# Re-ordering the steps of a fused layernorm, long-convolution and gated-GLU kernel

## The chip, the cores and the metric

The kernel runs on one core of a Trainium2 chip. Its time is the device time of one execution in microseconds (us); the figure for a kernel is the median of several executions. Five engines work side by side on a core: PE (TensorE, matrix products), DVE (VectorE), ACT (ScalarE), POOL (GpSimd) and SP (SyncE, which here issues nearly all the transfers). Each has a queue of instructions of its own and works it off strictly in order; semaphores hold an instruction back until what it needs is done. The profile also shows PEld, the loading of weights into TensorE, and the DMA engines that move the data.

## The reference

The input has 2048 rows and 640 channels, in bf16. Cut to what matters:

```python
xn = layernorm(A_q)                                   # over the 640 channels
# A: a shift convolution and a long convolution, per channel
k_shift[t] = sum over m<4 of k[t-m] * shift_k[:, m]
kv = k_shift * v
y  = irfft(rfft(kv, 4096) * rfft(ssm_k, 4096))[:2048] + kv * ssm_D
A  = xn * y
# B: a gated GLU, 640 -> 1728 -> 640
B  = (sigmoid(xn @ w_gate) * (xn @ w_up)) @ w_down
out = A_q + A + B
```

## The kernel before, in words

**Rows and the GLU.** Row 16p + b lies on partition p, in block b (16 blocks of 128 rows). Blocks form four groups t of 512 rows. For a group, the layernorm runs on DVE (`ln_norms`, `ln_var`, `ln_xn`, lines 192 to 219) and POOL (`ln_pow`), and four transposing transfers (`xn_turn`, line 240) write xn, turned, into the one buffer `xnT`. (Group 0 is turned on PE.) Then 13 pairs of `gate_mm` and `up_mm` (line 260, five matmuls each, 128x512) and one `both_mm` (line 281) follow. ACT takes the sigmoid of the gate product (`gate_ev`, line 269; `both_ev`, line 287), and DVE multiplies it with the up product into `hT` (`up_ev`, line 275). Each result lies in one of four PSUM buffers, the pool psG (tag g), and a product must wait until the buffer of four products earlier has been read. At the end of a group stand 16 steps of `down_mm` (line 304, seven matmuls each), two to a result, and `down_ev` (line 309, DVE) adds that into `x`, from which the output is stored.

**The convolution.** It is done in five chunks c of 128 channels, as a two-stage Fourier transform by small matrices. For a chunk:

- `load_k`, `load_halo`, `load_v`, `load_taps`, `load_h` fetch its inputs. `load_h` (lines 134 to 139) fills `hn`, of which there is one buffer, so `load_h(c)` can go only when `h_turn(c-1, ·)` (line 323, DVE, a transposition) has read it.
- `kv_op(c, 0..15)` (lines 330 to 346, DVE) does the shift convolution and the product with v, into `kvh` (two buffers).
- `st1_mm(c, 0..7)` (lines 363 and 365) is the first stage on PE, eight matmuls each, into the pool psC (two PSUM buffers, tag c). `st1_ev` copies the result to an SBUF tile `t1` (two buffers, each for two results): by ACT (line 223) or by DVE (line 226).
- `wr1(c, 0..3)` (line 377) writes a full `t1` to a table in DRAM, 512 KB, "d<-t" in the profile. The `t1` buffer comes free when that write has landed. So `st1_ev(c, 4)` waits for `wr1(c, 0)`, `st1_ev(c, 6)` for `wr1(c, 1)`, and `st1_ev(c+1, 0)` for `wr1(c, 2)`.
- `rd2(s)` (line 387) reads the table back in another layout for each of four subgroups s = 4c to 4c+3; `st2_mm(s)` (line 396) is the second stage and needs both psC buffers; `st2_ev(s, 0..1)` copies both to the slot s mod 3 of `xz`; `prod(s, 0..1)` (lines 409 and 411, DVE: a shuffle, then a product) is the product of the two spectra.
- `inv1_mm(y)` (line 425, 32 matmuls, both psC buffers), y = 2c and 2c+1, takes two slots of `xz` for the way back; its read of slots 2y mod 3 and (2y+1) mod 3 goes by a stride over the slots between them. `inv1_ev(y, 0..1)` copies its results to `ao`, `wr2` (lines 441 and 445) and `rdb` (line 455) go through DRAM once more.
- `inv2_mm(c, 0..3)` (line 464, eight matmuls, a psG buffer each) is the last stage; `inv2_q` (line 469) multiplies by xn and `inv2_x` (line 474) adds to `x`, both on DVE.

**What sets the order.** The program is scheduled by hand. All steps stand in `chains`, one list for each letter, each in its natural order; the string `ORDER` is read letter by letter, and each letter emits the next step of its list. The letters:

| letter | step | engine |
|---|---|---|
| g | gate_mm, up_mm, both_mm, down_mm | PE |
| a, b, c, d | st1_mm, st2_mm, inv1_mm, inv2_mm | PE |
| s | gate_ev, both_ev | ACT |
| u | up_ev, both_mul, down_ev | DVE |
| A, B, C | st1_ev, st2_ev, inv1_ev by ACT | ACT |
| I, F, J | the same three by DVE | DVE |
| k, H, l, q, p | kv_op, h_turn, layernorm, inv2_q and inv2_x, prod | DVE |
| t | taps (from chunk 1) | ACT |
| D, P, Z | add_D, ln_pow, taps(0) | POOL |
| m, n, h, K, V, T | loads (weights and chunks 0 and 1; x and a table; then h, k, v, taps of later chunks) | SP |
| w, r, W, R, e, o | wr1, rd2, wr2, rdb, xn_turn, store | SP |

```python
    left = {k: iter(v) for k, v in chains.items()}
    for k in "".join(ORDER.split()):
        fn, args = next(left[{"F": "B", "J": "C", "I": "A", "Y": "E"}.get(k, k)])
        fn(*args, **({"copy": dve_copy} if k in "FJIY" else {}))
```

An engine thus runs its own letters in the order of the string. What the string says of letters of different engines against each other only sets which buffer use comes first and which dependencies arise. SP is one queue for all the letters of its rows: a transfer that has to wait there holds the issues behind it.

Of the kernel before, what the change touches and what calls it, by code (L numbers as in the profile page):

```python
# [57 lines left out]
def kernel(  # L58
# [569 lines left out]
    step("o", store, NB - 1, NB, 4 * P, DM)  # L628

    ORDER = """  # L630
    mgmmmmgmgmgsummZmgmgsmmgugmssgkmmukgskgugkusgsugkkgkHggmmuskuggkHmssukgmDgggukskgukkksaTmmgauAgmkaAH
    HlglAalAlglmwgautAkagugmggPmwlkgAhglkelauleggkakukkugekAAuuDkHgkuaaekgkwgsATKugkAwgsnkkgskgtuKaKAuka
    gskkgauwgkAlDAakVgglkKkrsakAuwAgakgVsAgalswAkaguKgkkAurbgkBswksHgTBgkbtuguBBpkgawkgslaAgsuKkalupKgrA
    AgkahPlnHsAwugaglVasgkgVpAsTAKukDpuckwglkkCgaCaHAugkAkgkeklubkgrkBBgguuwkgbggkpghtBBrbkegleBgBaauegw
    HAparguVkApauAkgwpADWaugakksAngkugpkwlAsucgsgJlpkCulbrgBKBsgaAuapgpAgrbsFggBussWkukrlpcHgguPCCgbslkV
    ggBuBgbpslBkuBRdpgspgWqqcusdgCgkrkkrCsbqFugqBgubskgBRdwBuagpAaqAdgllWwrsewRpugaqgIaggrpAaAaqupgIqupg
    ddcCgeuqgJebgupegFRuBgqbBpgqBgWpdcrguqqgJqCrubwuwdrgFpBgsbqpggpWpqBugBpscsuJggCurpgbggRFBbsWpdsudupq
    rgBqgqBcqRJsgrpCgsbBuWguBpdspqgbuBBgpqdpsgcgrugCRJqbpggsduBqsBgupgspgWqRqcuJdqgsgCdoqgusqWgudggqgugo
    uRgquRggddouqqgguqddgqqqqoquqggoogouoogouoooo
    """  # L640
    left = {k: iter(v) for k, v in chains.items()}
    for k in "".join(ORDER.split()):
# [33 lines left out]
```

## Time and profile before

| | |
|---|---|
| median of 3 runs | 238.03 us (237.77 to 238.77) |
| the profiled execution: its time, its span | 237.94 us, 236.16 us |
| granted TensorE clock | 1.00 |
| PE busy | 229.1 us, 97% of the span |
| DVE busy | 204.1 us, 86% |
| ACT busy | 121.7 us, 52% |
| POOL busy | 11.5 us, 5% |
| moved by DMA | 56.79 MB, mean 240 GB/s |

The span is the time from the first to the last instruction in the trace of the slowest core; the rest of the execution's time lies around it. In a line of a timeline the columns are start and length in us, engine, line of the kernel, operation, what it writes and reads by the program's tile names, its shape and how many instructions the row holds; in brackets stands how long the engine was idle before and what it waited for. A matmul's end is modelled and overlaps the next one's start, so a step's cost on PE is read from start to start. A line of a window has its bounds and length, the busy time and instruction count of PE, PEld, DVE, ACT and POOL in this order, the granted clock, the share of the DMA engines and GB/s. A line of the waits has the engine and the instruction that waited, what it waited for, the total in us, how many times, and the longest. A line of the DMA issues has the transfer, the queue, how many, the size, and the median time from issue to landing in us. SP's "SPq" rows show an issue's start and how long the issuing took, not the transfer.

### The profile page before, as it was taken

The page shows a single profiled execution, that of the slowest core. Times are in us where ns is not written, and L with a number is a line of the kernel's source. Part 1 is how long each engine was busy: PE and PEld are TensorE (multiplying, and loading weights), DVE is VectorE, ACT ScalarE, POOL GpSimd, SP SyncE. Part 2 cuts the span into 40 slices and gives each one's busy share as a digit, 9 for nine tenths or more (in the row PEclk, how much of TensorE's full clock was granted, in tenths as well). Part 3 has the DMA queues.
Part 4 walks back from the last instruction along what each step waited for, and adds up shares of the span by engine and source line. Part 5 has one row for each costly group of instructions (what it writes and reads, how often), then busy time and mean ns, then how long its engine had stood idle before and what let it go on. Part 6 is the DMA issues. An engine that isn't in the chain of part 4 may idle for free.

```text
span 236.2 us, 5433 instructions
## 1 busy us (share of the span) xinstructions
PE 229.1 (97%) x2205; PEld 131.2 (56%) x2205; DVE 204.1 (86%) x364; ACT 121.7 (52%) x152; POOL 11.5 (5%) x24
## 2 busy tenths in 40 slices
PE   7799999999899899999999999999999999999995
PEld 3664445877355445666754444478664344446772
DVE  3632898999969999999999999899999999988473
ACT  2343323633564897776776777653346367653000
POOL 5210000020100001000100010000000000000000
PEclk9999999999999999999999999999999999999999
DMA  6999999958899999899899996899989879556664
GB/s 211 292 313 237 259 308 299 257 174 163 223 317 269 321 253 270 225 286 217 228 232 321 248 265 186 240 246 271 235 260 284 238 186 255 160 155 177 191 212 134
DMA packets 97183, 56.79 MB, mean 240 GB/s; under 512 B 55878, under 2 KB 91270, under 8 KB 96902
## 3 DMA queue, kind: packets, MB, share of 16 engines
q1 hardware_dynamic: 96214, 55.62, 90.3%
q10 hardware_dynamic: 944, 0.82, 1.1%
q8 instruction: 17, 0.28, 0.5%
q14 instruction: 8, 0.07, 0.1%
HBM read 36.12 MB, written 18.35 MB: 231 GB/s over the span
## 4 chain that ended last, share of the span: by engine, by line
PE 84%; DVE 8%; DMA 4%; issue 1%; ACT 0%; ACTq 0%; DVEq 0%
PE pg L260 23%; PE pu L260 23%; PE pd L304 20%; PE psb L464 4%; PE ps L396 3%; DMA w<-in_B_w_up_dram 3%; PE ps L363 3%; PE ps L365 3%; PE psa L425 2%; PE pg L281 1%; DVE st L198 1%; DVE tmp L341 1%; DMA xnT<-xn 1%; DVE acc L343 1%; PE pu L251 1%
## 5 line engine op out<-in xcount | busy, mean ns | idle before, releaser
L260 PEld LDWEIGHTS <-w 128*128 128x128 bf16 x500 | 46.5, 98 | 55.8 <-issue 6.8
L304 PE MATMUL pd<-wd,hT 128*128 128x320 bf16 (+2 forms) x448 | 65.3, 299 | 0.0
L260 PE MATMUL pg<-xnT,w 128*128 128x512 bf16 x250 | 62.2, 380 | 0.9 <-DMA xnT<-xn 0.9
L260 PE MATMUL pu<-xnT,w 128*128 128x512 bf16 x250 | 62.2, 380 | 0.8 <-DVE hT L275 0.8
L304 PEld LDWEIGHTS <-hT 128*128 128x128 bf16 x448 | 41.9, 98 | 18.2 <-issue 2.3
L223 ACT CAST t<-ps 128x1024 bf16<-128x1024 f32 x38 | 37.8, 1016 | 23.6 <-PE ps L365 16.0
L269 ACT ACTIVATE sig<-pg 128x512 bf16<-128x512 f32 x52 | 31.1, 603 | 30.7 <-PE pg L260 27.7
L223 ACT CAST xz<-ps 128x1024 bf16<-128x1024 f32 x35 | 34.2, 1015 | 20.3 <-PE ps L396 20.3
L275 DVE TENSOR_TENSOR hT<-sig,pu 128x512 bf16<-128x512 bf16 x52 | 34.8, 675 | 9.6 <-PE pu L260 5.6
L411 DVE TENSOR_TENSOR xz<-xz 128x2048 bf16<-128x2048 bf16 x20 | 24.3, 1215 | 0.1
L365 PE MATMUL ps<-kvh,S1t 128*128 128x128 bf16 x160 | 21.7, 220 | 0.0
L363 PE MATMUL ps<-kvh,S1t 128*128 128x128 bf16 x160 | 21.6, 218 | 0.0
L341 DVE TENSOR_TENSOR tmp<-kx,sc 128x1024 bf16<-128x1024 bf16 x30 | 20.5, 683 | 0.4
L343 DVE TENSOR_TENSOR acc<-acc,tmp 128x1024 bf16<-128x1024 bf16 x30 | 20.5, 684 | 0.4
L309 DVE TENSOR_TENSOR x<-pd,x 128x320 bf16<-128x320 f32 (+2 forms) x32 | 15.2, 483 | 5.9 <-PE pd L304 5.7
L363 PEld LDWEIGHTS <-S1t 128*128 128x128 bf16 x160 | 15.5, 97 | 2.8 <-DVE kvh L346 0.3
L365 PEld LDWEIGHTS <-S1t 128*128 128x128 bf16 x160 | 15.4, 96 | 2.6
L198 DVE BATCH_NORM_STATS2 st<-x 128x6 f32<-128x320 bf16 x32 | 13.9, 476 | 2.7 <-DMA x<-in_A_q_dram 2.7
L469 DVE TENSOR_TENSOR yx<-psb,xn 128x512 bf16<-128x512 f32 x20 | 13.7, 684 | 1.4 <-PE psb L464 1.0
L409 DVE STREAM_SHUFFLE xz<-xz 128x512 f32<-128x512 f32 x20 | 14.5, 725 | 0.0
L223 ACT CAST ao<-psa 128x1024 bf16<-128x1024 f32 x11 | 10.8, 1014 | 5.8 <-PE psa L425 5.6
L464 PEld LDWEIGHTS <-TBt 128*128 128x128 bf16 x160 | 9.8, 98 | 3.0 <-issue 1.5
(48 smaller groups left out, 149.3 us busy)
## 6 DMA issues: line engine op xcount, KB each, us to landing
d<-t SPq DMA_DIRECT2D x20, 512.0 KB, 5.3
t<-d SPq DMA_DIRECT2D x20, 512.0 KB, 5.7
bi<-d SPq DMA_DIRECT2D x8, 512.0 KB, 4.8
d<-ao SPq DMA_DIRECT2D x6, 512.0 KB, 5.6
kx<-in_A_k_dram SPq DMA_DIRECT2D x10, 256.0 KB, 5.3
hn<-in_A_ssm_k_dram SPq DMA_DIRECT2D x20, 128.0 KB, 5.2
kvh<-in_A_v_dram SPq DMA_DIRECT2D x10, 256.0 KB, 5.4
x<-in_A_q_dram SPq DMA_DIRECT2D x3, 640.0 KB, 6.4
```

The lines of the kernel that those rows point to most:

```text
L198: nc.vector.bn_stats(d["st"][:, i, s2, :], x[:, b, s2 * 320:(s2 + 1) * 320])
L223: nc.scalar.copy(out=out, in_=in_)
L260: nc.tensor.matmul(pg[:, :], lhsT=w[:, c, u * UP + fc * P:u * UP + (fc + 1) * P], rhs=xnT[:, :, c, :], start=(c == 0), stop=(c == NC - 1))
L269: nc.scalar.activation(sig[fc][:, :], pgs[0, fc][:, :], ACT.Sigmoid)
L275: nc.vector.tensor_tensor(hT[:, fc, :], sig[fc][:, :], pgs[1, fc][:, :], ALU.mult)
L304: nc.tensor.matmul(pd[:, :], lhsT=hT[:, fc, bb * P:(bb + 1) * P], rhs=wd[:, fc, es], start=(fc == 0), stop=(fc == NFC - 1))
L341: nc.vector.tensor_tensor(d["tmp"][:, :, :], kx[:, lo + 3 - m:hi + 3 - m, :], sb(m), ALU.mult)
L343: nc.vector.tensor_tensor(d["acc"][:, :, :], d["acc"][:, :, :], d["tmp"][:, :, :], ALU.add)
L363: nc.tensor.matmul(ps[:, i, 0:P], lhsT=S1[:, b, h, :], rhs=cin[c]["kvh"][:, 0, b, :], start=True, stop=True)
L365: nc.tensor.matmul(ps[:, i, P:2 * P], lhsT=S1[:, b, h, :], rhs=hp[:, b // 2, b % 2, :], start=True, stop=True)
L411: nc.vector.tensor_tensor(z[:, 1:3, :, :], z[:, 0:1, :, :].to_broadcast((P, 2, 8, P)), z[:, 1:3, :, :], ALU.mult)
L464: nc.tensor.matmul(ps[:, i, :], lhsT=TB[:, h, 4 * m + i, :], rhs=bi[:, h, 4 * (m % 2) + i, :], start=(h == 0), stop=(h == 1))
```

## The change

Only the string `ORDER` differs; the steps, their code, their sizes and their number are the same.

```diff
     ORDER = """
-    mgmmmmgmgmgsummZmgmgsmmgugmssgkmmukgskgugkusgsugkkgkHggmmuskuggkHmssukgmDgggukskgukkksaTmmgauAgmkaAH
-    HlglAalAlglmwgautAkagugmggPmwlkgAhglkelauleggkakukkugekAAuuDkHgkuaaekgkwgsATKugkAwgsnkkgskgtuKaKAuka
-    gskkgauwgkAlDAakVgglkKkrsakAuwAgakgVsAgalswAkaguKgkkAurbgkBswksHgTBgkbtuguBBpkgawkgslaAgsuKkalupKgrA
-    AgkahPlnHsAwugaglVasgkgVpAsTAKukDpuckwglkkCgaCaHAugkAkgkeklubkgrkBBgguuwkgbggkpghtBBrbkegleBgBaauegw
-    HAparguVkApauAkgwpADWaugakksAngkugpkwlAsucgsgJlpkCulbrgBKBsgaAuapgpAgrbsFggBussWkukrlpcHgguPCCgbslkV
-    ggBuBgbpslBkuBRdpgspgWqqcusdgCgkrkkrCsbqFugqBgubskgBRdwBuagpAaqAdgllWwrsewRpugaqgIaggrpAaAaqupgIqupg
-    ddcCgeuqgJebgupegFRuBgqbBpgqBgWpdcrguqqgJqCrubwuwdrgFpBgsbqpggpWpqBugBpscsuJggCurpgbggRFBbsWpdsudupq
-    rgBqgqBcqRJsgrpCgsbBuWguBpdspqgbuBBgpqdpsgcgrugCRJqbpggsduBqsBgupgspgWqRqcuJdqgsgCdoqgusqWgudggqgugo
-    uRgquRggddouqqgguqddgqqqqoquqggoogouoogouoooo
+    mmmmmmmggggsmmsugggsugmmZmksukukgmkksgggumkgmmsumgkgsugHkmgssuHDkkmgkumgmsggkTksgukgKmuksggukgguuala
+    glAgmaAmwaAtlgllagkgPukmAAKgwllkKlkalukgeggeHakgkgkkuekAkageDAuuaAwuHAagskggkmgusggkuwsggknhkTalgruA
+    gAlHHsutsKuakggKklVAagwkksukwgTgAagsglruAVDskaAkakwhgAkkKsugkskaaAkAgugkblkuPHBgkwsBpuwngDtgbsBBrgrk
+    spgallukHauAAgVaAggaskAuaggwkagApTelkAkgepcweukluCgkKkCkgKwVlaAkagukguAkkhbggekuBkBgKbtgurkVBgaBupaw
+    glkAHgpAbsgpugkpBagBrWkwnaAusuAgpaAarAglsglcgkCCglsbuwDpskkuBWBggkakrsPpkpAuaggAsubgFBpgcuwkCJRgrgbs
+    gsHBugpdkBWburpqskgrpguBlgBcqVdRsgkCCpgqbsBuguFskgbBpkguwldqBasgaIgWarugArAwpdlaeueRlqaeApgguAgcgguJ
+    CqbwgBBgqadqppuerAgbdgWpuqwBBgpgqcqCgugppRrJubgqdgFBbsuWrpdqpgBRqguqBcJsugCgrpsbggpduqdqBsBuWqbBBrgs
+    ppgqpgcggJsCugsRbuBgudBrpqsgdqpgqquqbBgpsgBgWsucgCRrdgCsbpBugpgqudgRsFqpdpuqscJoCggdqWWqousRggqugggg
+    ouuqggRuoqgugoodudqqqgogdqqqdqqgugggouuoooooo
     """
```

What comes out of it on each engine, where the prediction speaks of it:

- SP, around the second group's transposes. Before: wr1(0,1), load_h(2), xn_turn(1,0..3), wr1(0,2), load_taps(2), load_halo(2), wr1(0,3), load_x(2), load_k(2,·), wr1(1,0), load_v(2,0,8), load_halo(3), rd2(0), wr1(1,1), load_v(2,8,16), wr1(1,2). After: wr1(0,1), load_k(2,8,16), xn_turn(1,0..3), wr1(0,2), load_v(1,8,16), wr1(0,3), load_x(2), load_h(2), load_taps(2), rd2(0), load_halo(3), load_k(3,0,8), load_v(2,0,8), wr1(1,0), wr1(1,1), load_taps(3), rd2(1), load_v(2,8,16), wr1(1,2).
- DVE, in the same stretch. Before: h_turn(1,0) and h_turn(1,1) ahead of ln_norms(1,·). After: h_turn(1,1) behind down_ev(0,3,1). Before, kv_op(2,0) stands ahead of up_ev(1,4), after, behind it.
- PE, chunk 1 to 2. After: st2(1), gate(1,12), up(1,12), st1(2,2), st1(2,3), both(1), st1(2,4), two down, st1(2,5), st1(2,6), two down, st1(2,7), two down, inv1(0). Before: st1(2,2), up(1,10), st1(2,3), gate(1,11), st1(2,4), up(1,11), gate(1,12), st1(2,5), up(1,12), st1(2,6), both(1), st1(2,7), two down, inv1(0).
- PE, chunk 4. Before: st1(4,3), inv2(0,3), two down, st1(4,4), down, st1(4,5), two down, st1(4,6), st1(4,7), two down, inv2(1,0), inv2(1,1), inv1(4). After: st1(4,3), down, st1(4,4), down, inv2(0,3), st1(4,5), st1(4,6), three down, inv1(4).
- PE and DVE, group 3. Before, PE: st2(15), gate(3,4), up(3,4), st2(16), inv2(2,0), inv2(2,1), gate(3,5), up(3,5), inv1(7); DVE: prod(15,1), inv2_q and inv2_x (2,0), the same (2,1), inv1_ev(7,0), prod(16,0). After, PE: st2(15), gate(3,3), up(3,3), inv2(2,0), inv2(2,1), st2(16), gate(3,4), up(3,4), gate(3,5), inv1(7); DVE: inv2_q(2,0), up_ev(3,3), inv2_x(2,0), prod(15,0), prod(15,1), inv2_q(2,1), prod(16,0).
- Copies by DVE. Before, 14: inv1_ev(1,0), st2_ev(6,0), st2_ev(9,0), st1_ev(4,4), st1_ev(4,7), inv1_ev(4,1), st2_ev(11,0), inv1_ev(5,0), st2_ev(13,0), inv1_ev(6,0), st2_ev(15,0), inv1_ev(7,0), inv1_ev(8,1), inv1_ev(9,0). After, 11: st2_ev(6,0), inv1_ev(2,1), st2_ev(9,1), st1_ev(4,2), inv1_ev(4,0), inv1_ev(5,1), st2_ev(13,0), inv1_ev(6,0), inv1_ev(7,0), st2_ev(19,1), inv1_ev(9,0). The rest are ACT's.
- POOL's order is the same.

## The prediction

> **What bounds the kernel now.** I read the page first: the busy shares, then the slices, then the windows of five stages, and after those the waits and the timelines of PE, ACT and SP.
>
> ```profile
> span 236.2 us, 5433 instructions
> PE 229.1 (97%) x2205; PEld 131.2 (56%) x2205; DVE 204.1 (86%) x364; ACT 121.7 (52%) x152; POOL 11.5 (5%) x24
> d<-t SPq DMA_DIRECT2D x20, 512.0 KB, 5.3
> 58.00:82.00 24.00, 22.30 (x162) 12.32 (x160) 21.43 (x39) 13.84 (x18) 0.72 (x1) 1.00 0.96 277
> 82.00:104.00 22.00, 22.00 (x219) 12.65 (x219) 21.71 (x38) 17.10 (x22) 1.43 (x2) 1.00 0.97 250
> 104.00:178.00 74.00, 74.00 (x855) 43.07 (x853) 71.57 (x126) 46.54 (x55) 2.17 (x2) 1.00 0.99 250
> ...
> ACT t L223 <- DMA d<-t: 6.9, 5, 2.6
> ...
> 60.05 1.24 PE L260 MATMUL pg<-xnT,w 128*128 128x512 bf16 x5 [0.93 <-DMA xnT<-xn]
> ...
> 77.73 1.24 PE L260 MATMUL pu<-xnT,w 128*128 128x512 bf16 x5 [0.77 <-DVE hT L275]
> ```
>
> PE is the bound. In the window 104 to 178 it is busy 74.00 of 74.00 us, and its granted clock is 1.00. So until the last matmul at 233.28, only PE's pauses can be won; behind it a tail of 2.88 us (last down_ev, last stores) closes the span. PE's pauses behind its first long product (14.39) sum to 2.30 us, counted from one step's start plus its usual length to the next step's start: 1.09 at 60.05 (gate_mm(1,0) waits for the transpose of xn), 0.93 at 77.73 (up_mm(1,6) waits for a PSUM buffer that up_ev frees), 0.13 at 79.38 (st1_mm(2,1), held by an ACT copy) and 0.15 at 102.16 (st1_mm(3,0), held by kv_op). The wait of ACT for "d<-t", a first-table write that must land before its SBUF buffer t1 can be refilled, costs PE almost nothing today; it matters below.
>
> ```profile
> 58.73 0.54 SPq L377 DMA_DIRECT2D d<-t  x1
> 64.90 3.03 SPq L377 DMA_DIRECT2D d<-t  x1
> ...
> 62.41 1.93 ACT L223 CAST t<-ps 128x1024 bf16<-128x1024 f32 x2 [0.49 <-DMA d<-t]
> 71.88 1.01 ACT L223 CAST t<-ps 128x1024 bf16<-128x1024 f32 x1 [1.67 <-DMA d<-t]
> ...
> 191.42 1.22 DVE L411 TENSOR_TENSOR xz<-xz 128x2048 bf16<-128x2048 bf16 x1
> 192.56 0.68 DVE L469 TENSOR_TENSOR yx<-psb,xn 128x512 bf16<-128x512 f32 x1
> 193.27 0.42 DVE L474 TENSOR_TENSOR x<-x,yx 128x512 bf16<-128x512 bf16 x1
> 196.01 0.72 DVE L409 STREAM_SHUFFLE xz<-xz 128x512 f32<-128x512 f32 x1
> ```
>
> The first two rows are SP issuing wr1, the next two ACT resuming on its landing: 62.41 − 58.73 = 3.7 us and 71.88 − 64.90 = 6.9 us (3.0 of it in the issue). Rows of later writes give 5.6, 5.0 and 5.9, the page's median is 5.3. The DVE rows are the durations used below.
>
> **The change part by part.** Every product, copy and transfer stays (56.79 MB); only positions move, so the cost is pauses won and made. PE step lengths, start to start in its timeline: gate, up or both product 1.08 (60.05 to 61.13), seven down matmuls 0.95, st1_mm 0.45, st2_mm 0.37, inv2_mm 0.45 (146.57 to 147.03), plus 0.09 where a quarter-array product follows a full one. An ACT copy is 1.01, two together 1.92.
>
> *Removed.* (1) The transposes xn_turn(1,·) move on SP ahead of load_h(2), whose issues take 2.35 us (50.90): the 1.09 goes. What is late next is gate_mm(1,0) itself, in PE order. (2) On DVE up_ev(1,4) now stands before kv_op(2,0), which in the old trace started at 69.21 after 1.73 idle for "kx": the 0.93 goes. (3) The 0.13 and 0.15 go with it, as their neighbours are re-ordered. Sum −2.30.
>
> *Added, S1.* inv1_mm(7) reads xz slots 0 and 2 with a stride that spans slot 1, so it is held by any write to slot 1 issued before it. Now prod(16,0) is ahead of it on DVE; before, it was behind. From the end of inv2_mm(2,0): DVE does inv2_q .68, up_ev .67, inv2_x .42, the shuffle .72, the product 1.22, inv2_q .68, the shuffle of 16 .72 = 5.11; six joins overlap by .08 but for one dependent one (+.03), −.37; it begins .24 in: 4.98. PE in that time: inv2_mm .45, st2_mm(16) .46, three products 3.24, .09 = 4.24. Pause about 0.75. Behind inv1_mm stand all of PE's products.
>
> *Added, S2.* inv1_mm(4) needs both psC buffers, the second freed by ACT's copy of st1(4,6), which waits for wr1(4,1). From the end of st1_mm(4,3): result .16, start .04, copy 1.01, issue .02, landing 5.3, .03, copy 1.01, .04 = 7.61. PE meanwhile: five down steps 4.75 in all, st1_mm three times 1.35, inv2_mm .45, .09 = 6.64. Pause 0.97; nothing at a landing of 4.33, 1.57 at 5.9. In the old order two more inv2_mm and two more down steps, and st1_mm(4,7), lay between.
>
> *Added, S3.* inv1_mm(0) likewise waits for ACT's copies of st1(2,6) and (2,7) behind wr1(2,1). From the start of st1_mm(2,3): .20, two copies 1.92, .05, landing 5.3, .04, two copies 1.92 = 9.43. PE: st1_mm five times 2.25, both_mm 1.08, six down steps 5.70, .09 = 9.12. Pause 0.31; nothing at 5.0, .91 at 5.9.
>
> *Added, S4.* The SP queue around 58 to 72 is re-ordered, and what was behind the moved step waits: load_h(2) now stands between wr1(0,3) and wr1(1,0). h_turn(1,1), which frees load_h's one buffer hn, moves on DVE from about 44 to behind down_ev(0,3,1), about 61.2. Then SP: load_h(2) with a landing about 6.5 (rows of load_h: 50.55 to 56.08 is 5.5, 84.77 to 93.23 is 8.5), two halo issues, a k and a v load, wr1(1,0) at about 70.4, landing 75.7. ACT's copies and the sigmoid behind it (1.01 + .60 + 1.01) reach 78.2; wr1(1,2) lands near 83.5; two copies give 85.5, against PE, whose step lengths bring it to st2_mm(0) at 85.34: 0.16.
>
> *Costed at nothing.* Three copies move from DVE to ACT (14 on DVE become 11): ACT +3 × 1.01, hidden since ACT is 52% busy; DVE −3 × 1.22, no gain since PE is already 74.00 of 74.00 busy where they lie. If ACT's cover failed, one copy late would be 1.0 on the next psC user. POOL's order is the same. The stores and rdb moved late keep about 12.7 us between rdb(4,0) and its inv2_mm: tail 2.88 as before. load_k, load_v and load_x moved among SP's issues: not priced one by one, for no row shows the new queue. SP issues in order, so such a pause can be 0, or as long as the two that this queue made before, 1.09 + 0.93 = 2.0. I take 0.5, nearer nothing, since in the whole old trace only those two pauses of PE go back to a late transfer; a gain is excluded, for the pauses removed are all there were.
>
> Sum: −2.30 + 0.75 + 0.97 + 0.31 + 0.16 + 0.5 = +0.4 on the profiled execution's 237.94 (span 236.16, 1.78 around it). The median of the runs is 238.03, 0.09 above: 237.94 + 0.4 + 0.09 = 238.4.
>
> **The rivals.** *Short landings.* If the writes of S2 to S4 land like the row at 58.73, in 3.7, those pauses and the queue's vanish: −2.30 + 0.75 = −1.55, 236.5. For it: that row. Against: the median 5.3, and a DMA share of 0.96 to 0.99 where the three stand. Chance 0.18. The Trainium skill, page "DMA: Bandwidth & Descriptors", section "Anatomy of one DMA — SWDGE (gpsimd) path", gives about 2.0 us fixed plus the bytes at 436 GB/s, measured on GpSimd's queue; for 512 KB I estimate 3.2 us from it, and the sum would be −1.55 too. The trace disagrees: 5.3 in the median.
>
> *A late write (the other side).* In S4 wr1(1,0) stands behind load_h(2). If load_h lands as the row of 8.5 instead of 6.5 (+2.0), or wr1(1,0) as the 6.9 instead of 5.3 (+1.6), ACT's gate_ev(1,6) and the copies of st1(2,·) come late and PE stops at gate_mm(1,8) (slack .8) and st2_mm(0) (no slack). The price is 1.5 to 3.5 beyond the sum, 239.5 to 241.5, about 240.5. For it: DMA share 0.96 there, and ACT already waits 1.67 and 2.62 for d<-t at 71.88 and 76.92. Against: ACT idles over a third of that window. It decides from 1.1 us of lateness. Chance 0.27.
>
> *The pauses move.* The transposes come earlier, but what follows fills the time: DVE, busy 21.43 of 24 in that window, is late at the next up_ev, so half of the 2.30 stays: 238.4 + 1.1 = 239.5. Chance 0.10. Against: DVE had 1.73 idle at 69.21.
>
> **How the numbers follow.** Forecast 0.45 (its own range 237.3 to 239.1: without the queue's 0.5, S2 and S3 at landings of 5.0 give −0.72, at 5.9 +1.09), short landings 0.18, late write 0.27, pauses moved 0.10. What a measurement can tell from no change is 0.5%, 1.2 us: 236.84 to 239.22. Short landings are faster; the forecast is the same but for .01; a late write is slower; pauses moved are slower: faster 0.18, same 0.44, slower 0.38. The range takes in both and is cut inside them, at 236.7 (landings near 4.5, by S2 and S3) and 241.2 (the late write short of its full 3.5), which leaves out about 1 in 10 on each side.
>
> **What would show it.** Right: no PE wait on "xnT<-xn" near 59, none on "hT L275" near 77; waits of about 0.7 at inv1_mm(7) (L425, for DVE xz), about 1.0 at inv1_mm(4) and 0.3 at inv1_mm(0) (for ACT). S4 is seen in ACT's "t L223 <- DMA d<-t" around 68 to 84. The prediction is wrong if the wait for d<-t grows well past 6.9 us in sum with PE waits at L396 or L260 behind it (late write), or if the L425 waits are missing (short landings).

## The result, and the profile after

The changed kernel takes 240.74 us in the median of four executions (240.39 to 241.31); the kernel before took 237.90 in four (237.63 to 238.77) beside it. The ratio is 1.0115, with a 95% interval of 1.0082 to 1.0148: slower by more than the 0.5% that the prediction set as the least that can be told from no change. The forecast was 238.4, inside the 0.5%; its range of 236.7 to 241.2 held the time. In a later session the same two kernels stood closer: 239.88 against 239.33, a ratio of 1.0031 (1.0000 to 1.0061). The experiments show what differs between executions. The ratios, and the spreads named below, leave out the few executions over 1.5% above the fastest of the same kernel.

The profiled execution of the changed kernel took 240.75 us, 1.8 around its span. The head of its page:

```profile
span 239.0 us, 5435 instructions
PE 230.3 (96%) x2204; PEld 132.1 (55%) x2205; DVE 200.8 (84%) x361; ACT 124.3 (52%) x155; POOL 13.2 (6%) x24
```

Three of its windows, with the bounds used before the change (PE, PEld, DVE, ACT, POOL busy, then clock, DMA share, GB/s):

```profile
58.00:82.00 24.00, 24.00 (x162) 13.01 (x160) 23.62 (x44) 13.35 (x19) 0.42 (x1) 1.00 0.98 267
82.00:104.00 22.00, 21.58 (x222) 12.93 (x220) 21.05 (x37) 16.27 (x22) 2.10 (x2) 1.00 1.05 245
104.00:178.00 74.00, 71.67 (x820) 41.35 (x818) 67.28 (x119) 49.89 (x59) 2.17 (x2) 1.00 0.99 249
```

And from its list of waits (total, times, longest), where ACT's wait for the first-table writes was 6.9 before:

```profile
ACT t L223 <- DMA d<-t: 8.0, 5, 2.7
```

The window 58 to 82, which held the two large pauses, is now full: PE 24.00 of 24.00 instead of 22.30. The window 104 to 178, where PE was never idle, now lacks 2.33 us. So the gain came, and more than that was lost behind it. Where, PE's timeline shows; these are its idle times behind the prologue, apart from one short one at 165:

```profile
102.33 0.65 PE L425 MATMUL psa<-xz,SMt 32*32 32x512 bf16 x30 [0.42 <-ACT t L223]
...
117.55 0.44 PE L396 MATMUL ps<-t,SMt 32*32 32x512 bf16 x16 [1.12 <-DMA t<-d]
...
127.06 0.39 PE L425 MATMUL psa<-xz,SMt 32*32 32x512 bf16 x2 [0.68 <-ACT t L223]
...
127.98 0.65 PE L425 MATMUL psa<-xz,SMt 32*32 32x512 bf16 x30 [0.53 <-ACT t L223]
...
195.60 0.66 PE L425 MATMUL psa<-xz,SMt 32*32 32x512 bf16 x32 [0.71 <-DVE xz L409]
```

Counted start to start, as in the prediction (an inv1_mm that waits for nothing takes 0.58 to the next step's start), the pauses are:

| place on PE | held by | predicted | before | after |
|---|---|---|---|---|
| gate_mm(1,0) | transposes of xn | gone | 1.09 | 0 |
| up_mm(1,6), st1_mm(2,1) | DVE, ACT | gone | 0.93 + 0.13 | 0 |
| st1_mm(3,0) | kv_op | gone | 0.15 | 0 |
| S4: st2_mm(0) | first-table write | 0.16 | 0 | 0 |
| S3: inv1_mm(0) | ACT, behind wr1(2,1) | 0.31 | 0 | 0.80 |
| st2_mm(4) | its table read rd2(4) | in the queue's 0.5 | 0 | 1.20 |
| inv1_mm(1) | ACT, behind wr1(3,1) | in the queue's 0.5 | 0 | 1.66 |
| S2: inv1_mm(4) | ACT, behind wr1(4,1) | 0.97 | 0 | 0.29 |
| S1: inv1_mm(7) | DVE's prod(16,0) | 0.75 | 0 | 0.78 |

The new ones sum to 4.73, the old ones to 2.30: 2.43 more. The start of the work on PE came 0.35 later in this execution (14.74 against 14.39), and the last matmul ended 2.82 later (236.10 against 233.28), which these two add up to within 0.04. The span is 2.81 longer (238.97 against 236.16), with the same tail. That accounts for the result. The two pauses that no line of the prediction named, 1.20 and 1.66, are together as large as the whole difference.

How both arise is seen in SP's timeline of the changed kernel, first, and in two rows of ACT's, second:

```profile
111.03 0.42 SPq L387 DMA_DIRECT2D t<-d  x1
111.50 2.49 SPq L169 DMA_DIRECT2D kvh<-in_A_v_dram  x1
114.09 1.24 SPq L377 DMA_DIRECT2D d<-t  x1
115.42 0.38 SPq L387 DMA_DIRECT2D t<-d  x1
115.86 1.33 SPq L441 DMA_DIRECT2D d<-ao  x1
117.28 3.96 SPq L377 DMA_DIRECT2D d<-t  x1
```

```profile
100.35 1.93 ACT L223 CAST t<-ps 128x1024 bf16<-128x1024 f32 x2 [2.42 <-DMA d<-t]
...
126.00 1.93 ACT L223 CAST t<-ps 128x1024 bf16<-128x1024 f32 x2 [2.71 <-DMA d<-t]
```

rd2(4) is the issue at 111.03. Its buffer was free when st2_mm(2) ended at about 108.2, but h, k and transposing loads stood ahead of it; it landed at 117.51. More than these issues held it: load_k(4,8,16), the last of them, was issued by 109.99, and for the remaining 1.0 us SP waited for the landing of load_v(3,8,16), issued at 104.62. In this order the two transfers signal their landing on the same semaphore, so the later one goes out only when the earlier one has landed. SP's list of waits, first, and the chain that ended last (start, length), second, have it:

```profile
SPq L387 <- DMA kvh<-in_A_v_dram: 1.0, 1, 1.0
```

```profile
104.62 6.34 DMA kvh<-in_A_v_dram
...
111.03 6.25 DMA t<-d
```

wr1(3,1) is the issue at 117.28. The copy it waits for ended at 115.95, and then SP was still busy with earlier issues and needed 3.96 us for this one. ACT got its buffer back at 126.0, and PE stood at inv1_mm(1) until the two copies were done.

### The profile page after: what moved, and what is told of

The parts are those of the page before. It is cut to its first block, busy times and chain, and to the rows that moved or that the text cites. A ratio compares the mean times of both kernels' runs of the same rounds, so it can differ in the third digit from the quotient of the medians.

```text
span 239.0 us, 5435 instructions
## 1 busy us (share of the span) xinstructions
PE 230.3 (96%) x2204; PEld 132.1 (55%) x2205; DVE 200.8 (84%) x361; ACT 124.3 (52%) x155; POOL 13.2 (6%) x24
## 4 chain that ended last, share of the span: by engine, by line
PE 78%; DMA 14%; ACT 3%; DVE 2%; issue 1%; SPq 0%; ACTq 0%
PE pu L260 21%; PE pg L260 20%; PE pd L304 19%; DMA d<-t 6%; PE psb L464 4%; DMA w<-in_B_w_up_dram 3%; PE psa L425 3%; DMA kvh<-in_A_v_dram 3%; DMA t<-d 3%; PE ps L365 3%; PE ps L363 3%; PE ps L396 2%; ACT t L223 2%; PE pg L281 1%; PE pu L251 1%
## 5 line engine op out<-in xcount | busy, mean ns | idle before, releaser
L223 ACT CAST t<-ps 128x1024 bf16<-128x1024 f32 x39 | 38.6, 1014 | 30.3 <-PE ps L365 19.7
L223 ACT CAST xz<-ps 128x1024 bf16<-128x1024 f32 x36 | 35.2, 1016 | 16.2 <-PE ps L396 16.2
L365 PE MATMUL ps<-kvh,S1t 128*128 128x128 bf16 x160 | 21.1, 219 | 0.0
L363 PE MATMUL ps<-kvh,S1t 128*128 128x128 bf16 x160 | 21.1, 217 | 0.0
L223 ACT CAST ao<-psa 128x1024 bf16<-128x1024 f32 x12 | 11.8, 1014 | 8.7 <-PE psa L425 7.8
```

The source lines that it names most:

```text
L223: nc.scalar.copy(out=out, in_=in_)
L363: nc.tensor.matmul(ps[:, i, 0:P], lhsT=S1[:, b, h, :], rhs=cin[c]["kvh"][:, 0, b, :], start=True, stop=True)
L365: nc.tensor.matmul(ps[:, i, P:2 * P], lhsT=S1[:, b, h, :], rhs=hp[:, b // 2, b % 2, :], start=True, stop=True)
```

## The experiments

Each edit moves letters in ORDER; it is shown by the order that it gives to the queue. The times of a call are compared with the kernel before on the same chip, where its executions spread more than in the four above (237.5 to 241.0), so a single pause of 1 us does not decide a median. The verdict on each pause is read from the profile. The expectations give some pauses of the changed kernel up to 0.15 smaller than the table (1.05 for 1.20, 1.55 for 1.66), by a less exact reading.

### The changed kernel and the kernel before, again

> The changed kernel itself, on the chip that runs the other three of this call. Theory (the pauses come from the order): the same five places pause, 102, 117, 127, 165 and 195, 4 to 5.5 in sum, and it is 2 to 3.5 slower than the kernel before on this chip. Rival (they came from one execution's slow transfers): two or more of the five are missing, and the difference is under 1.

Measured: 239.88 against 239.33, ratio 1.0031 (1.0000 to 1.0061). The profiled execution has the pauses at the same five places, as the theory said: 0.21, 0.30, 1.73, 0.49, 0.78. Their sum, 3.51, is less than the 4 expected, and the difference between the kernels, 0.55, is under 1, as the rival had it. So the places are of the order; the sizes are of the execution.

> The kernel before itself, profiled again on the chip of these runs, where its executions spread from 237.7 to 240.8. Theory (its pauses too are as long as transfers land late): the pauses at 60, 77.7, 79.4 and 102.2 stand at the same places, and in a slow execution one or more of them is longer than the 1.09, 0.93, 0.13, 0.15 first seen; the span follows their sum to 0.2. Rival (the spread lies outside PE's pauses): the pauses sum to 2.2 to 2.4 whatever the span.

Measured: 239.06 against 238.98. The profiled execution of the kernel before, one of its slower ones at 240.28 us, has in PE's timeline (four of five):

```profile
60.48 1.24 PE L260 MATMUL pg<-xnT,w 128*128 128x512 bf16 x5 [1.20 <-DMA xnT<-xn]
...
78.34 1.24 PE L260 MATMUL pu<-xnT,w 128*128 128x512 bf16 x5 [0.95 <-DVE hT L275]
...
101.24 0.65 PE L425 MATMUL psa<-xz,SMt 32*32 32x512 bf16 x32 [0.55 <-DVE xz L411]
...
104.38 0.23 PE L363 MATMUL ps<-kvh,S1t 128*128 128x128 bf16 x1 [0.47 <-DVE kvh L346]
```

Start to start these are 1.36, 1.11, 0.62 and 0.63, and with 0.63 at st1_mm(2,1), for ACT, 4.35 instead of 2.30, with a span of 238.5 instead of 236.2. The theory holds: the spread between these two executions is in the pauses, and the order before is open to it as the order after is. One pause, at inv1_mm(0), was not there at all in the first trace. So the ratio of the two kernels can differ between sessions; what makes the transfers of one execution land later than those of another is not shown.

### The pause at inv1_mm(7), S1

```diff
 DVE: ... prod(15,1), inv2_q(2,1),
-     prod(16,0), inv1_ev(7,0), up_ev(3,4)
+     inv1_ev(7,0), prod(16,0), up_ev(3,4)
```

> The changed kernel with one DVE step moved: prod(16,0) behind inv1_ev(7,0), as before the change. Theory (the pause of PE at inv1_mm(7) is there because the shuffle of subgroup 16 writes the xz slot that the strided read spans): the 0.80 pause goes whole, 240.7 becomes 239.9, and up_mm(3,5) follows inv1_mm(7) after 0.58. Rival (DVE is simply full there, so the next DVE step that PE needs is late instead): PE pauses as long at the next up or inv2 step, within 5 us; the time stays at 240.5 to 240.9.

Measured: 239.4, ratio 1.0015 (0.9986 to 1.0044). PE's timeline of this kernel there:

```profile
194.90 0.65 PE L425 MATMUL psa<-xz,SMt 32*32 32x512 bf16 x32
195.48 1.25 PE L260 MATMUL pu<-xnT,w 128*128 128x512 bf16 x5
```

The wait is gone, the next product starts 0.58 later, and no pause over 0.1 follows up to the last down steps. DVE was not the limit; the place of one shuffle was. The other pauses stand: 0.99, 0.81, 1.75 and 0.60, and 0.31 at S4.

### The late read, rd2(4)

```diff
 SP: ... load_h(4), xn_turn(2,3),
-    load_k(4,8,16), rd2(4), load_v(4,0,8), wr1(3,0)
+    rd2(4), load_k(4,8,16), load_v(4,0,8), wr1(3,0)
```

> The changed kernel with two SP issues exchanged: rd2(4) ahead of load_k(4,8,16). Theory (place in SP's queue: rd2(4) is issued 2.9 us after its buffer is free, since it stands behind other issues and their semaphore): it is issued at about 109.5 instead of 111.0, lands near 116 instead of 117.5, and PE's pause of 1.05 before up_mm(2,0) falls to 0.1 or less: 239.7. Rival (the DMA engines are full, so that an earlier issue lands no earlier): the landing stays at 117 to 117.5, the time at 240.5 to 240.9.

Measured: 240.47, ratio 1.0059 (1.0019 to 1.0100); the profiled execution took 239.54. SP's timeline of this kernel:

```profile
109.02 0.52 SPq L387 DMA_DIRECT2D t<-d  x1
109.77 0.67 SPq L155 DMA_DIRECT2D kx<-in_A_k_dram  x1
```

The read goes out at 109.02, and PE's pause at st2_mm(4), 1.20 before, is gone; the one at inv1_mm(1) stays, 1.67. The exchange did two things: rd2(4) no longer stands behind load_k(4,8,16), whose issue takes 0.6, and it no longer shares a semaphore with load_v(3,8,16). Now load_k does, and goes out at 109.77, when that load lands (109.76). Over eight traces, the four with rd2(4) in the place that the change gives it have it issued 0.06 or 0.07 us after the landing of load_v(3,8,16) each time, and pause 1.20, 0.30, 0.81 and 0.03; the four with it one place ahead, three of them with other edits too, do not pause. So the place in the queue made this pause, as the theory said, and by these issue times mostly through that landing. The time shows no gain: its executions ran from 239.1 to 241.9, and the ratio lies between the two of the changed kernel, so it does not measure one pause.

### The late write, wr1(3,1)

```diff
 SP: ... load_k(4,8,16), rd2(4),
-    load_v(4,0,8), wr1(3,0), rd2(5), wr2(0), wr1(3,1), TBt table
+    wr1(3,0), rd2(5), wr2(0), wr1(3,1), load_v(4,0,8), TBt table
```

> The changed kernel with one SP issue moved: load_v(4,0,8), not needed before 132, goes from ahead of wr1(3,0) to behind wr1(3,1). Theory (SP's queue is what holds the write: its issue began 1.3 us after the copy it waits for and took 3.96): wr1(3,1) is issued by 117 within 1 us, lands by 123, ACT's 2.71 wait for d<-t at 126.0 is gone, and PE's pause of 1.55 at inv1_mm(1) with it: 239.2. Rival (full DMA engines): wr1(3,1) still lands after 125, or the TBt table or rd2(6) is late in its place; 240.3 to 240.9.

Measured: 239.02, ratio 1.0004 (0.9969 to 1.0039). SP's timeline of this kernel, with wr2(0), wr1(3,1) and the load:

```profile
113.52 1.15 SPq L441 DMA_DIRECT2D d<-ao  x1
116.08 3.05 SPq L377 DMA_DIRECT2D d<-t  x1
119.18 0.43 SPq L169 DMA_DIRECT2D kvh<-in_A_v_dram  x1
```

PE's pause at inv1_mm(1) falls from 1.66 to 0.27 (it is 1.66 to 1.75 in the four traces with the old place): the write begins its issue at 116.08, as soon as the copy allows, and lands at 123.45. One part of the expectation failed: the issue still took 3.05, not under 1. And the pause at st2_mm(4) went too (0.03), though rd2(4) kept its place: it was issued at 110.63 in this execution, since load_v(3,8,16) had landed at 110.57, and landed at 116.44. Whether taking load_v from behind it also shortened its landing (5.8 against 6.5) this run alone cannot say.

### What removed the old pauses

```diff
 turns_first, SP of the kernel before:
-    wr1(0,1), load_h(2), xn_turn(1,0..3), wr1(0,2)
+    wr1(0,1), xn_turn(1,0..3), load_h(2), wr1(0,2)      (DVE: h_turn(2,0) behind kv_op(1,12))
```

> The kernel before with load_h(2) behind xn_turn(1,0..3) on SP, and h_turn(2,0), which needs it, four DVE steps later. Theory (the first removed pause was the place of load_h(2) alone): no PE wait for xnT at 60, the 1.09 goes whole and 238.0 becomes 236.9. Rival (the pauses move: DVE was nearly full and is late next): the 0.93 before up_mm(1,6) grows to 1.5 or more, 237.5 to 238.2.

Measured: 238.78, ratio 1.0001 (0.9969 to 1.0034). The pause at gate_mm(1,0) is gone; instead PE's timeline of this kernel has, among others:

```profile
74.18 0.22 PE L363 MATMUL ps<-kvh,S1t 128*128 128x128 bf16 x1 [0.85 <-ACT t L223]
...
78.66 1.24 PE L260 MATMUL pu<-xnT,w 128*128 128x512 bf16 x5 [1.25 <-DVE hT L275]
```

Start to start these are 1.01 and 1.41, with 0.53 at st1_mm(1,2) and 0.56 at st1_mm(3,0) beside them. The rival holds, though 1.41 is short of its 1.5: the 1.09 is won and lost again within 20 us. kv_op(2,0) started at 70.15, after 2.20 of idle, since load_k(2) was issued as late as before.

```diff
 k2_early, SP of the kernel before:
-    wr1(0,1), load_h(2), ..., load_halo(2), wr1(0,3), load_x(2), load_k(2,0,8), load_k(2,8,16)
+    wr1(0,1), load_halo(2), load_k(2,0,8), load_k(2,8,16), load_h(2), ..., wr1(0,3), load_x(2)
```

> The kernel before with load_halo(2) and both halves of load_k(2) moved on SP ahead of load_h(2), into the 3.3 us in which SP waited there. Theory (the second removed pause, 0.93 before up_mm(1,6), came from load_k(2) being issued at 62, late: kv_op(2,0) idled 1.73 for it and everything behind on DVE, up_ev(1,4) too, came late): kv_op(2,0) starts by 67.5, and the pauses at 77.7 and 79.4 (0.93 and 0.13) go; the 1.09 at 60 stays: 1.0 less than the kernel before on the same chip. Rival, the prediction's step as it stood (up_ev(1,4) standing behind kv_op(2,0) to (2,7) on DVE): 0.5 or more of the 0.93 stays.

Measured: 238.30, ratio 0.9959 (0.9930 to 0.9988). The pauses at up_mm(1,6) and st1_mm(2,1) are gone, with up_ev(1,4) where it was on DVE, as the theory said. But that does not show that the earlier load removed them, for the transposes came later, and PE waits longer at gate_mm(1,0), 2.29 instead of 1.09, by its timeline:

```profile
61.17 1.24 PE L260 MATMUL pg<-xnT,w 128*128 128x512 bf16 x5 [2.13 <-DMA xnT<-xn]
```

So PE came to up_mm(1,6) at 77.92, 1.12 later than it could have in the kernel before (77.73 less its wait of 0.93). DVE, which itself waited for that late PE, started kv_op(2,0) at 68.52, not by 67.5, and ended up_ev(1,4) at 77.51 instead of 77.67, only 0.16 earlier. The wait is gone in this run because the one who waited came later; what the earlier load is worth with PE on time it cannot say. The gain of 0.4% in time is not explained by it either: with 0.59 at st1_mm(3,0) the profiled execution has 2.88 of pauses, between the 2.30 and the 4.35 of the kernel before.

What removed the 0.93 in the change, its own DVE rows show. Before (kv_op(2,0), up_ev(1,4)), first, and after (up_ev(1,3) and (1,4), kv_op(2,0)), second:

```profile
69.21 0.69 DVE L337 TENSOR_TENSOR acc<-kx,sc 128x1024 bf16<-128x1024 bf16 x1 [1.73 <-DMA kx<-in_A_k_dram]
...
76.99 0.68 DVE L275 TENSOR_TENSOR hT<-sig,pu 128x512 bf16<-128x512 bf16 x1
```

```profile
70.61 1.26 DVE L275 TENSOR_TENSOR hT<-sig,pu 128x512 bf16<-128x512 bf16 x2
71.79 0.69 DVE L337 TENSOR_TENSOR acc<-kx,sc 128x1024 bf16<-128x1024 bf16 x1
```

load_k(2) had landed by 55.22 in the change, and still kv_op(2,0) began 2.6 later than before, since DVE was busy with other steps until then. up_ev(1,4) ended at 71.87 instead of 77.67 because it stands ahead of it. PE came to up_mm(1,6) at 74.69; kv_op(2,7), behind which up_ev(1,4) stood before, ended at 80.25. So in the change it was the place of up_ev(1,4), as the prediction's step (2) has it; this is read from the rows, and that place alone was not tried.

Both moves together, first with up_ev(1,4) moved as well:

```diff
 SP of the kernel before:
-    wr1(0,1), load_h(2), xn_turn(1,0..3), wr1(0,2)
+    wr1(0,1), load_halo(2), load_k(2), xn_turn(1,0..3), load_h(2), wr1(0,2)   (DVE: h_turn(2,0) behind kv_op(1,15))
 before_fixed, DVE:
+    up_ev(1,4) ahead of ln_norms(2,1)
```

> The kernel before with load_halo(2) and load_k(2) ahead on SP, then xn_turn(1,0..3), then load_h(2); h_turn(2,0) on DVE behind kv_op(1,15); up_ev(1,4) ahead of ln_norms(2,1). Theory (the two removed pauses come from the places of load_h(2) and load_k(2) in SP's queue, and nothing of the rest of the change is needed to remove them): no pause of PE over 0.4 between 58 and 82, and 1.5 to 2.2 less than the kernel before on the same chip. Rival (in that window DVE is full, 21.4 of 24, and a PE that comes 2 us sooner waits for kv_op): pauses of 1 or more in sum come back between 65 and 104, and the time is within 0.9 of the kernel before.

In this kernel up_ev(1,4) stands ahead of gate_ev(1,4) and multiplies with the sigmoid of an earlier block, which it need not wait for; that part of its computation is changed. Measured: 239.26, ratio 0.9998 (0.9966 to 1.0029). Its profiled execution, 237.31, has neither old pause, but 0.71 at st1_mm(1,4), which waits for ACT behind a first-table write, and 0.63 at st1_mm(3,0), and the time is that of the kernel before: the rival holds. With all of the computation, up_ev(1,4) in its old place:

> The kernel before with SP's queue alone re-ordered at one place: load_halo(2) and load_k(2) first, then xn_turn(1,0..3), then load_h(2); and h_turn(2,0), which waits for the last, behind kv_op(1,15) on DVE. Theory (both removed pauses are places in SP's queue): no pause over 0.1 at gate_mm(1,0) nor at up_mm(1,6); some comes back at st1_mm(1,4) to (1,6), 0.9 for wr1, and at st1_mm(3,0), 0.7 for kv_op, as in the kernel with the same moves; 0.6 less than the kernel before. Rival (the place of up_ev(1,4) on DVE is needed too): 0.5 or more at up_mm(1,6).

Measured: 238.54, ratio 0.9965 (0.9929 to 1.0000). The profiled execution, the longest of the ten (240.06, at a granted clock of 0.993), has at most 0.1 at gate_mm(1,0), 0.33 at up_mm(1,6), which is between the theory and its rival, and 0.75 + 0.46 at st1_mm(1,2) and st1_mm(1,3), again for ACT behind the writes. So SP's order alone takes the first old pause away. Of the second a third stays, with PE already 1.21 behind by the two new pauses; in the kernel with up_ev(1,4) moved as well there was none. In the change itself nothing came back there (window 58 to 82: 24.00 of 24.00), which takes the rest of its re-ordering; which part of it was not tried.

### All five treated

```diff
 the changed kernel, with the three edits above (S1, rd2(4), load_v(4,0,8)) and
 SP: -  rd2(5), wr2(0), wr1(3,1)
     +  rd2(5), wr1(3,1), wr2(0), load_v(4,0,8)
 PE: -  st1(2,7), down, down, inv1(0), down, down, st1(3,0), st1(3,1), down, down, st2(2)
     +  st1(2,7), down, down, down, inv1(0), down, down, st1(3,0), st1(3,1), down, st2(2)
     -  st1(4,6), down, down, down, inv1(4), down, down, st2(11), down
     +  st1(4,6), down, down, down, down, inv1(4), down, down, st2(11)
```

> The changed kernel with all its five pauses treated: prod(16,0) behind inv1_ev(7,0); rd2(4) ahead of load_k(4,8,16); load_v(4,0,8) and wr2(0) behind wr1(3,1); inv1_mm(0) and inv1_mm(4) one down step later each, with the next down step moved up behind them. Theory (five separate pauses, each with its own place): 0.80 + 1.05 + 1.2 + 0.7 + 0.2 = 4.0 less than the changed kernel, 1.2 to 1.8 less than the kernel before on the same chip. Rival (where one goes the next stands: DVE and the DMA engines have no room): half of it or less, so no less than the kernel before.

Measured: 237.53, ratio 0.9931 (0.9905 to 0.9957): faster than the kernel before and than the changed one (1.0031 in the same call). Its executions lie within 237.22 to 238.14. All five pauses are gone, but others stand at st2_mm(2) (0.72, for ACT's copy of st1(3,1)), st2_mm(13) (0.68, for DVE's copy inv1_ev(5,1)) and, with 0.3 or less each, at three more places. So 2.4 of the theory's 4.0 came, against the 239.88 of the changed kernel, and part of the rest moved. SP's timeline of this kernel, with wr1(3,1), wr2(0) and the load:

```profile
115.75 0.34 SPq L377 DMA_DIRECT2D d<-t  x1
116.14 0.43 SPq L441 DMA_DIRECT2D d<-ao  x1
116.61 3.36 SPq L169 DMA_DIRECT2D kvh<-in_A_v_dram  x1
```

wr1(3,1), ahead of wr2(0) now, is issued in 0.34 us instead of 3.96 or 3.05; the long issue has gone to the load behind wr2(0), which nobody waits for.

```diff
 after_best: as above, but
 PE: st1(2,7), down, down, down, inv1(0), down, st1(3,0), st1(3,1), down, down, st2(2)
     and st2(13) behind gate(3,0)
```

> The changed kernel with the five pauses treated as in the kernel above of 237.5, but the down step left where it was between st1_mm(3,1) and st2_mm(2), and st2_mm(13) one product later. Theory (its 0.72 at st2_mm(2) and 0.68 at st2_mm(13) are places on PE): both fall to 0.3 or less, 0.9 less: 236.5 to 236.8 and a span near 235. Rival (DVE and the DMA engines are behind these pauses): they stand at the next steps, and the time stays at 237.3 to 237.7.

Measured: 237.35, ratio 0.9929 (0.9902 to 0.9956), no different from the one above. Those two pauses went, and 0.31 + 0.46 came at st1_mm(3,0) and st1_mm(3,1), for ACT's copies of inv1(0), and 0.83 in sum between 187 and 190, for a table read and an rdb. The rival holds.

> The changed kernel with three of its five pauses treated (prod(16,0) behind inv1_ev(7,0); rd2(4) ahead of load_k(4,8,16); load_v(4,0,8) and wr2(0) behind wr1(3,1)) and inv1_mm(0) and inv1_mm(4) left where the change puts them. Theory (those two pauses are places that a later inv1_mm takes away): they stand at 0.25 to 1.0 and 0.15 to 0.9, and the time is 0.9 to 1.3 above the 237.5 of the kernel with all five treated, 238.4 to 238.8, by the same comparison with the kernel before. Rival (that edit only moves the pauses to st2_mm(2) and st2_mm(13), 0.72 and 0.68 there): the time is within 0.4 of it, 237.2 to 237.9.

Measured: 237.51, ratio 0.9942 (0.9917 to 0.9968). The pauses at inv1_mm(0) and inv1_mm(4) stand in the profiled execution (1.05 and 0.56), as the theory said, but the time is not above that of the kernel with all five treated, as the rival said. By time, the two edits of the PE order brought nothing that these intervals can tell; the three on SP and DVE carry the gain.

## Why the prediction was right or wrong

**The removed 2.30.** Right: all four pauses are gone in the first trace of the changed kernel and in its second. Step (1) is borne out by the kernels with load_h(2) behind the transposes, step (2) by DVE's rows in the change; why the 0.13 and 0.15 went was not tried.

**S1, 0.75.** Right: 0.78, and 0.77 to 0.78 in the other runs that keep it. The sum of DVE's rows was the pause.

**S2, 0.97, and S3, 0.31.** The mechanism was right and the landing was the size that was off. Over six traces that keep both places, by the landing of the write ahead:

| run | wr1(2,1) landing | pause at inv1_mm(0) | wr1(4,1) landing | pause at inv1_mm(4) |
|---|---|---|---|---|
| changed | 5.71 | 0.80 | 4.55 | 0.29 |
| changed, again | 5.13 | 0.21 | 4.75 | 0.49 |
| s1_undone | 5.91 | 0.99 | 4.85 | 0.60 |
| rd2_ahead | 5.59 | 0.68 | 5.15 | 0.90 |
| load_v_behind | 5.62 | 0.70 | 4.69 | 0.44 |
| three_fixed | 5.96 | 1.05 | 4.82 | 0.56 |

Each pause is the landing minus a constant, 4.92 and 4.26 to within 0.01, where the prediction had 4.99 and 4.33. One landing for both, 5.3, was the error: the first write lands near 5.7, the second near 4.8.

**S4, 0.16.** None in either trace of the changed kernel, and 0.24 to 0.31 in four of its variants. h_turn(1,1) ended at 61.56 (61.2 predicted), and wr1(1,0) landed at 74.1 (75.7). The rival of the late write at this place did not happen; the time of 240.7 lies where that rival put it, for another cause. So it is luck that the range held the time: its upper end came from this rival, not from the term that grew.

**The queue, 0.5.** This is the step that failed: 1.20 and 1.66, 2.86 in sum, and beyond its own upper end of 2.0. The other four terms together came out 0.3 smaller than forecast (1.87 for 2.19). "Nearer nothing, since in the whole old trace only those two pauses of PE go back to a late transfer" took what one trace of the old order showed for a property of the kernel. Two SP stretches around 108 to 118 were not worked through as S4 was: rd2(4) stood behind load_h(4), a transposing load and load_k(4,8,16) and, by a shared semaphore, behind the landing of load_v(3,8,16), and wr1(3,1) behind load_v(4,0,8) and wr2(0). Moving one issue each removed 1.20 and 1.39.

**The rest.** Three copies more on ACT cost nothing that a trace shows. The tail is as before. The rival of short landings did not come: the median of the writes to d is 5.6 and 5.1 in the two traces of the changed kernel, where it was 5.3 before. The 3.2 estimated from the Trainium skill, page "DMA: Bandwidth & Descriptors", section "Anatomy of one DMA — SWDGE (gpsimd) path", stays as far off. The rival of the moved pauses came in the kernels that took the old pauses away alone, not in the change.

## What to carry to other kernels

Where one queue issues nearly all transfers in order, a re-ordering must be priced issue by issue: for each read or write that an engine waits for, when its buffer is free, what stands ahead of it, and how long those issues take. A pause that hangs on a landing should be written as the landing minus a constant, with the landing of that place, not of the median row. What holds an issue can also be a semaphore that it shares with an earlier transfer, so the landing of that one belongs in the price. And a pause removed on the path is kept only if what feeds the next steps comes earlier too: one of the edits here won 1.09 and gave it back within 20 us. When a wait is gone, it is worth looking whether what was waited for came earlier or the one who waited came later.

## What the runs showed of the hardware that was not expected

How long SP takes for an issue depends on what it issued just before. In the first trace of the kernel before, an issue that followed within 0.3 us took 0.43 us in the median behind wr1 (17 issues), but 1.67 behind load_k (8), 1.32 behind load_v (4) and 1.97 behind a whole wr2 (6). The spread is wide: 0.27 to 1.60, 0.52 to 3.03, 1.10 to 2.27 and 1.06 to 4.12. load_k, load_v and wr2 move pieces of 256 bytes, wr1 runs of 4 KB on the writing side. With wr2(0) ahead of it wr1(3,1) took 3.96 and 3.05, and with wr2(0) behind it 0.34, while the load that then stood behind wr2(0) took 3.36. That the number of pieces is the reason was not tried by itself.

The same program's pauses differ between executions by 2.05 us, 2.30 and 4.35 for the kernel before, at a clock of 1.00 in both; the medians of the two kernels differ by 2.84 in the first session and by 0.55 in the later one.
